# Moving the weighted-sum matmuls ahead of the second tile's transposes in each pair of attention steps

## The chip, the cores and the metric

The kernel runs on one core of a Trainium2 chip. The metric is the device time of one execution in microseconds (us). Each number of a comparison is a median over several timed runs. A profile comes from one further execution under the hardware profiler; it has a time of its own and a span (first to last instruction of the program), and all times inside the trace are counted from the span's start.

The engines are named as the profile names them: PE (matmuls) with PEld (the weight loads that go with them), DVE, ACT, POOL, and SP, which only issues DMAs here.

## The reference

The computation has two parts, one feeding the other. The first is attention whose mask comes from hashing: 4 batches with 8 heads each, 768 tokens, head size 64.

```python
q_bits = (einsum('bhsd,dk->bhsk', q, proj) > 0)      # 6 bits a token, k_bits likewise
mask = q_bucket[:, :, :, None] == k_bucket[:, :, None, :]
scores = scale * matmul(q, k.transpose(0, 1, 3, 2))
scores = where(mask, scores, -1e9)
attn = exp(scores - scores.max(-1)); attn = attn / (attn.sum(-1) + 1e-9)
attn_out = matmul(attn, v)                           # [4, 8, 768, 64]
```

The second is a mixture of 8 experts over the 3072 tokens of the attention's output (512 features): each token goes to the expert with the largest logit, through `relu(x @ w1[e]) @ w2[e]` with 1024 hidden features, and is scaled by two gate values.

## The kernel before

**Stages.** The attention runs first, as 192 *steps*. One step is one tile of 128 query rows of one head against all 768 keys. Twelve steps make a pair of heads, six of them half of its rows (three query tiles of each head). Routing of a batch (which token goes to which expert) is computed beside the next batch's attention; the experts' matmuls follow behind the attention.

**One step** consists of these parts, spread over several turns of the loop:

- *Scores* (`scores`, lines 528 and 532). PE makes 4 matmuls with 384 columns into one of two `ps_s` buffers; DVE copies the tile to `sc`, clipped, and takes each row's minimum (the scores carry a negative sign).
- *Exponential* (`soft`, line 540). ACT, in place in `sc`, with the row sums added up on the side.
- *Normalising* (`normal`, lines 547 to 550), once for two steps: DVE prepares the reciprocal of the row sums (`rsum`), POOL multiplies both tiles by it.
- *Transposes* (`transposed`, lines 561 and 562). PE turns the six 128x128 blocks of the tile, three into each of two `ps_t` buffers, and ACT copies each buffer to `pts`.
- *Weighted sums* (`weighted`, line 572). For one block `c` of 128 keys and half a pair of heads, the product of `v` with the transposed weights, one matmul for each head. The head's 64 columns fill half of the array: head 0 goes to the first 64 output rows of `ps_a`, head 1 to the other 64, and the two stand side by side. The trace shows each as two records, so the two blocks that belong to a pair of steps make eight records. Behind block 5, DVE copies `ps_a` to `ot` (line 575).

**What sets the order.** The loop is written out by hand and every engine takes its instructions in the order in which the loop issues them (`manual_schedule`); nothing reorders them later. The loop goes in pairs of steps (`GROUP = 2`). In the turn for steps s0 and s0+1 it issues the scores of these two, the transposes of s0-4 and s0-3 (`LAG = 4`), and two blocks of weighted sums, planned in the table `products`. A second table, `at`, holds what else is due behind a step: splitting and projecting the next heads, loading, the routing, and early pieces of the experts' stage. Weighted sums of a half begin two turns after its last scores, with the first blocks of `products` at step 10 and the last at step 195, so 93 turns have some.

In the text a turn's two tiles are called the first and the second: first scores, first transposes, second scores, second transposes, weighted sums is the order on PE before the change.

**Buffers that tie the engines together.** `ps_s` and `ps_t` have two buffers each. So second transposes cannot start before ACT's copies of the first transposes, and scores cannot start before DVE has read the tile of two steps earlier. `sc` has six buffers, `pts` two for each head.

Of the kernel before, what the change touches and what calls it, by code (L numbers as in the profile page):

```python
# [44 lines left out]
GROUP = 2  # L45
# [13 lines left out]
def lsh_attention_then_moe(  # L59
# [27 lines left out]
    def signed():  # L87

        for h, s in ((0, 1.0), (1, -1.0)):
            hs = slice(h * D, (h + 1) * D)  # L90
            c = 2 * NB * h
            nc.gpsimd.tensor_scalar(pjc[hs, c:c + NB], pj[hs, 0:NB], s, 0.0, ALU.mult, ALU.add)
            nc.gpsimd.tensor_scalar(pjc[hs, c + NB:c + 2 * NB], pj[hs, 0:NB], -s, 0.0, ALU.mult, ALU.add)
# [95 lines left out]
    def w2_piece(pool, r, f, idle=""):  # L189
        raw = load_weights([P, 2, DM], w2[bass.ds(expert[r], 1), :, f:f + 2].rearrange("e p f d -> p (e f) d"))  # L190
        hi, lo = split_weights(pool, "w2", NFB // 2, [P, 2, DM], raw, idle)
        return [(hi[:, j], lo[:, j]) for j in range(2)]
# [108 lines left out]
    def new_h():  # L301
        return [ep.tile([P, NFB, CAP], F32R, name=n) for n in ("hh", "hl")]
# [10 lines left out]
    def up(w1s, xs, hs, fs, n):  # L313

        ph = ps_s.tile([P, 2, 512], F32, name="ps_s")[:, 0:len(fs), 0:n]
        for j, f in enumerate(fs):
            fc = slice(f * P, (f + 1) * P)
            product(ph[:, j], [(wh[:, fc], wl[:, fc]) for wh, wl in w1s],
                    [(xs[0][:, cc, 0:n], xs[1][:, cc, 0:n]) for cc in range(NCC)])
        hh, hl = (h[:, fs[0]:fs[-1] + 1, 0:n] for h in hs)  # L320
        nc.scalar.activation(hh, ph, AF.Relu)  # L321
        return lambda: nc.vector.scalar_tensor_tensor(hl, ph, 0.0, f32(hh), ALU.max, ALU.subtract)  # L322
# [44 lines left out]
    with ExitStack() as actx:  # L367
# [11 lines left out]
        at, products = {}, {}  # L379
# [8 lines left out]
        def load(g, heads=(0, 1)):  # L388
            st = pairs[g]
            st.setdefault("qk", [])  # L390
            for j in heads:
                t = hp.tile([P, S], F32, name="qk", bufs=4)
                nc.sync.dma_start(t, qkT[2 * g + j])
                st["qk"].append(t)

        def load_v(g):
            pairs[g]["v"] = tp.tile([P, 2, NT, D], F32, name="vt", bufs=2)
            nc.sync.dma_start(pairs[g]["v"], v[g])
# [71 lines left out]
        def first_low(part):  # L470

            st = pairs[0]
            xl, yl, xr, qk = st["xl"][1], st["yl"][1], st["xr"][1], st["qk"][1]
            if part == 0:
                nc.vector.tensor_tensor(xr[D:P], qk[D:P], f32(xl[D:P]), ALU.subtract)
                nc.gpsimd.tensor_scalar(xl[D:P], qk[0:D], -0.125, 0.0, ALU.mult, ALU.add)  # L476
            else:
                nc.vector.scalar_tensor_tensor(yl[0:D], qk[0:D], -0.125, f32(xl[0:D]), ALU.mult, ALU.subtract)
# [41 lines left out]
        def scores(s):  # L520
            g, hf, t, j = tile_of(s)
            st = pairs[g]
            qs = slice(t * P, (t + 1) * P)
            ss = ps_s.tile([P, 2, 512], F32, name="ps_s")
            kb = D + 2 * NB
            for l, r, k, first in ((st["xl"][j], st["xr"][j], P, True), (st["yl"][j], st["yr"][j], kb, False)):
                for n in range(2):
                    nc.tensor.matmul(ss[:, n, 0:HS], l[0:k, qs], r[0:k, n * HS:(n + 1) * HS],  # L528
                                     start=first, stop=not first)
            sc = tp.tile([P, 2, HS], F32, name="sc", bufs=LAG + 2)  # L530
            mn = sp.tile([P, 1], F32, name="mn")
            nc.vector.tensor_scalar(sc, ss[:, :, 0:HS], MASKED, None, ALU.min, ALU.min, accum_out=mn)  # L532
            return sc, mn

        def soft(s, sc, mn):
            if s % GROUP == 0:
                sums[s // GROUP] = sp.tile([P, GROUP], F32, name="rsum")
            pr = sc.rearrange("p a b -> p (a b)")
            k = s % GROUP
            nc.scalar.activation(pr, pr, AF.Exp, bias=mn, scale=-1.0,  # L540
                                 accum_out=sums[s // GROUP][:, k:k + 1])
            return pr

        def normal(s0):

            rs = sums.pop(s0 // GROUP)
            nc.vector.tensor_scalar(rs, rs, 1e-9, None, ALU.add)
            nc.vector.reciprocal(rs, rs)  # L548
            for k in range(GROUP):
                nc.gpsimd.tensor_scalar(live[s0 + k], live[s0 + k], rs[:, k:k + 1], 0.0, ALU.mult, ALU.add)  # L550

        def transposed(s, pr):
            g, hf, t, j = tile_of(s)
            hb, t = s // 6, t - 3 * hf
            if s % 6 == 0:
                blocks[hb] = [tp.tile([P, NT, HS], F32, name=f"pts{n}") for n in range(2)]
            pts = blocks[hb][j]
            for h in range(2):
                tr = ps_t.tile([P, 3, P], F32, name="ps_t")
                for c in range(3):  # L560
                    nc.tensor.transpose(tr[:, c], pr[:, (3 * h + c) * P:(3 * h + c + 1) * P], ident)  # L561
                nc.scalar.copy(pts[:, 3 * h:3 * h + 3, t * P:(t + 1) * P], tr)  # L562
# [153 lines left out]
        for g in range(NP):  # L716
            s0 = 12 * (g - 1)
# [28 lines left out]
        s0 = 12 * (NP - 1)  # L746
# [91 lines left out]
        with tc.manual_schedule(engines=MANUAL):  # L838
            load(0)
            load(1)  # L840
            load_v(0)
            make_identity(nc, ident)

            idle = ps_t.tile([P, 3, P], F32, name="ps_t")

            def turn_idle(n):
                for i in range(n):
                    nc.tensor.transpose(idle[:, i % 3], ident, ident)

            turn_idle(14)  # L850
            first_heads()
            turn_idle(4)
            live = {}
            for s0 in range(0, NSTEP + LAG, GROUP):
                for s in range(s0, s0 + GROUP):
                    if s < NSTEP:
                        live[s] = scores(s)
                    if s < 2:
                        first_low(s)
                    if s == 1:  # L860
                        signed()
                    if 0 < s < 3:
                        turn_idle(6)
                    if s == s0 and 0 <= s - GROUP < NSTEP:
                        normal(s - GROUP)
                    if 0 <= s - LAG < NSTEP:
                        transposed(s - LAG, live.pop(s - LAG))
                    if s < NSTEP:
                        live[s] = soft(s, *live[s])
                    for fn in at.get(s, ()):  # L870
                        fn()
                for s in range(s0, s0 + GROUP):
                    for fn in products.get(s, ()):
                        fn()


            hctx.close()
            ep = ctx.enter_context(tc.tile_pool(name="ep", bufs=1, side="right", reuse_waits="tile"))
            hs = new_h()
            w2s = []  # L880
            lows = []

            def fill(f):
                lows.append(up(early["w1"], early["x"], hs, [f], CAP0))

            def low():
                lows.pop(0)()

            fill(0)
            for f in range(0, NFB, 2):  # L890
                w2s += w2_piece(ep, 0, f, "hl")
            for c in range(NT):
                weighted(2 * NP - 1, c)
                if c == 0:
                    rows(NP - 1, 0, False)
                if c == 2:
                    r["add_pair"](0, lp)
            fill(1)
            low()
            r["add_pair"](1, lp)  # L900
            fill(2)
            r["best"]()
            low()
            r["choose"]()
            rows(NP - 1, 1, False)
            fill(3)
            low()
            r["prefix"]()
            fill(4)
            r["gates"]()  # L910
            low()
            r["ranks"]()
            fill(5)
            low()
            fill(6)
            r["cols"]()
            low()
            fill(7)
            r["hot"]()
            r["table"]()  # L920
            low()
            r["entries"]()
            gid0 = lead_slots(EARLY)
            low()
# [205 lines left out]
```

## Time and profile before

| what | value |
|---|---|
| median of 3 timed runs | 796.67 us (796.37 to 797.16) |
| profiled execution: its time | 791.77 us |
| profiled execution: its span | 790.0 us |
| PE busy | 770.3 us, 98% of the span |
| DVE, ACT, POOL busy | 61%, 58%, 48% |

The attention takes about the first 462 us, the experts the rest. A matmul's end in the trace is modelled: matmuls overlap in the pipeline, and the time that one really costs is the distance from its start to the start of the next.

### The profile page before, as it was taken

How to read it: one execution, taken by the hardware profiler on the slowest of the kernel's cores; microseconds unless marked ns; L12 is line 12 of the kernel's file. 1: busy time of each engine (PE TensorE's matmuls, PEld its weight loads, DVE VectorE, ACT ScalarE, POOL GpSimd, SP SyncE). 2: the span in 40 equal slices, each digit the busy share in tenths (PEclk: the TensorE clock that was granted, in tenths of full speed). 3: DMA queues.
4: the chain of work that ended last, by engine and by line, in shares of the span. 5: the costliest groups of instructions: out<-in, count | busy, mean ns of one | idle time of the engine just before them, and what ended most of it. 6: DMA issues, size and time to landing. Idle time of an engine off the chain costs nothing. (4 is left out here: it accounts for less than half of the span.)

```text
span 790.0 us, 13715 instructions
## 1 busy us (share of the span) xinstructions
PE 770.3 (98%) x4690; PEld 608.1 (77%) x4690; DVE 479.7 (61%) x1032; ACT 459.1 (58%) x934; POOL 382.1 (48%) x422
## 2 busy tenths in 40 slices
PE   7999999999999999999999999999999999999997
PEld 6777676667676767676767658878999999988895
DVE  6676667796766896675896737236363636454640
ACT  6877777777777777777768721234151525353331
POOL 7555544444543444544445892372627273746201
PEclk9999999999999999999999999999999999999999
DMA  5554454464565456455456152363444444445601
GB/s 170 135 135 88 101 128 86 118 140 85 120 145 130 81 126 143 91 123 129 88 123 166 54 137 62 106 217 124 144 147 150 152 150 148 150 150 179 220 24 39
DMA packets 84800, 98.90 MB, mean 125 GB/s; under 512 B 57999, under 2 KB 59439, under 8 KB 84720
## 3 DMA queue, kind: packets, MB, share of 16 engines
q1 hardware_dynamic: 79376, 84.58, 41.1%
q0 software_dynamic: 5200, 13.31, 5.1%
q8 instruction: 40, 0.66, 0.3%
q14 instruction: 40, 0.33, 0.1%
q10 hardware_dynamic: 144, 0.02, 0.0%
HBM read 59.49 MB, written 13.11 MB: 92 GB/s over the span
## 5 line engine op out<-in xcount | busy, mean ns | idle before, releaser
L550 POOL TENSOR_SCALAR sc<-sc,rsum 128x768 f32<-128x768 f32 x192 | 178.9, 945 | 218.1 <-DVE rsum L548 85.8
L532 DVE TENSOR_SCALAR_CACHE_REDUCE sc<-ps_s 128x768 f32<-128x768 f32 x192 | 183.3, 955 | 96.4 <-PE ps_s L528 88.4
L562 ACT COPY pts<-ps_t 128x384 f32<-128x384 f32 x384 | 164.4, 481 | 95.5 <-PE ps_t L561 95.0
L540 ACT ACTIVATE sc<-sc,mn 128x768 f32<-128x768 f32 x192 | 181.4, 945 | 15.2 <-DVE sc L532 14.3
L561 PE MATMUL ps_t<-ident,sc 128*128 128x128 f32 x1152 | 158.4, 273 | 3.9 <-POOL sc L550 1.8
L561 PEld LDWEIGHTS ps_t<-ident,sc 128*128 128x128 f32 x1152 | 137.2, 141 | 14.3 <-POOL sc L550 4.6
L572 PE MATMUL ps_a<-pts,vt 128*64 128x384 f32 x768 | 144.8, 499 | 0.0
L528 PE MATMUL ps_s<-xr,xl 128*128 128x384 f32 x384 | 117.1, 386 | 2.4 <-POOL xl L476 2.2
L528 PEld LDWEIGHTS ps_s<-xr,xl 128*128 128x128 f32 x384 | 57.9, 190 | 71.0 <-issue 33.6
L528 PE MATMUL ps_s<-yr,yl 76*128 76x384 f32 x384 | 100.0, 341 | 0.6 <-POOL yr L438 0.5
L322 DVE SCALAR_TENSOR_TENSOR hl<-ps_s,hh 128x256 fp32r<-128x256 f32 (+8 forms) x40 | 34.0, 849 | 109.0 <-ACT hh L321 88.3
L311 PE MATMUL ps_s<-xh,w1h 128*128 128x256 f32 (+7 forms) x288 | 97.8, 340 | 2.2 <-DVE hl L322 2.1
L311 PE MATMUL ps_s<-xh,w1l 128*128 128x256 f32 (+7 forms) x288 | 96.2, 334 | 0.8 <-DVE w1l L177 0.5
L311 PE MATMUL ps_s<-xlo,w1h 128*128 128x256 f32 (+7 forms) x288 | 96.0, 333 | 0.0
L285 POOL DMA_INDIRECT xq<-x_dram,idx x75 | 82.5, 1099 | 21.6 <-issue 21.1
L328 POOL DMA_INDIRECT out_dram<-yo,sid x29 | 30.6, 1056 | 116.4 <-ACT yo L327 69.2
L572 PEld LDWEIGHTS ps_a<-pts,vt 128*64 128x64 f32 x768 | 46.7, 136 | 50.4 <-issue 47.7
L321 ACT ACTIVATE hh<-ps_s 128x256 fp32r<-128x256 f32 (+8 forms) x40 | 29.1, 727 | 90.4 <-PE ps_s L311 75.6
L528 PEld LDWEIGHTS ps_s<-yr,yl 76*128 76x128 f32 x384 | 70.4, 190 | 1.2 <-POOL yr L438 1.2
L311 PEld LDWEIGHTS ps_s<-xh,w1h 128*128 128x128 f32 x288 | 54.9, 191 | 5.8 <-DVE hl L322 3.0
L311 PEld LDWEIGHTS ps_s<-xh,w1l 128*128 128x128 f32 x288 | 54.8, 190 | 2.6 <-DVE w1l L177 0.9
L311 PEld LDWEIGHTS ps_s<-xlo,w1h 128*128 128x128 f32 x288 | 54.9, 190 | 1.1
(204 smaller groups left out, 1020.6 us busy)
## 6 DMA issues: line engine op xcount, KB each, us to landing
w_raw<-in_w_dram SPq DMA_DIRECT2D x36, 512.0 KB
qk<-in_qkT_dram SPq DMA_DIRECT2D x32, 384.0 KB
xh<-in_w_dram SPq DMA_DIRECT2D x14, 512.0 KB
xlo<-in_w_dram SPq DMA_DIRECT2D x14, 512.0 KB
vt<-in_v_dram SPq DMA_DIRECT2D x16, 384.0 KB
xr<-xl SPq DMA_DIRECT2D x30, 192.0 KB
yr<-xl SPq DMA_DIRECT2D x30, 192.0 KB
xr<-yl SPq DMA_DIRECT2D x30, 192.0 KB
```

The costliest lines, as they stand in the source:

```text
L285: nc.gpsimd.indirect_dma_start(out=xq[:, k * P:(k + 1) * P], out_offset=None, in_=x_dram.rearrange("n (a f) -> (n a) f", a=NB32), in_offse ...
L311: nc.tensor.matmul(ps, l, r, start=first and k == 0, stop=last and k == len(pairs) - 1)
L321: nc.scalar.activation(hh, ph, AF.Relu)
L322: return lambda: nc.vector.scalar_tensor_tensor(hl, ph, 0.0, f32(hh), ALU.max, ALU.subtract)
L328: nc.gpsimd.indirect_dma_start(out=out[:, :], out_offset=bass.IndirectOffsetOnAxis(ap=sid[0:n, r, a:a + 1], axis=0), in_=yo[0:n], in_offse ...
L528: nc.tensor.matmul(ss[:, n, 0:HS], l[0:k, qs], r[0:k, n * HS:(n + 1) * HS], start=first, stop=not first)
L532: nc.vector.tensor_scalar(sc, ss[:, :, 0:HS], MASKED, None, ALU.min, ALU.min, accum_out=mn)
L540: nc.scalar.activation(pr, pr, AF.Exp, bias=mn, scale=-1.0, accum_out=sums[s // GROUP][:, k:k + 1])
L550: nc.gpsimd.tensor_scalar(live[s0 + k], live[s0 + k], rs[:, k:k + 1], 0.0, ALU.mult, ALU.add)
L561: nc.tensor.transpose(tr[:, c], pr[:, (3 * h + c) * P:(3 * h + c + 1) * P], ident)
L562: nc.scalar.copy(pts[:, 3 * h:3 * h + 3, t * P:(t + 1) * P], tr)
L572: nc.tensor.matmul(st["av"][j * D:(j + 1) * D], st["v"][:, j, c], blocks[hb][j][:, c], start=(c == 0), stop=(c == NT - 1))
```

## The change

In the loop over a turn's two steps, the two blocks of weighted sums are issued in the second step, right behind its scores and ahead of its transposes. Before, they were issued behind the loop, after the second transposes and after whatever `at` holds for the second step.

```diff
                     if s == s0 and 0 <= s - GROUP < NSTEP:
                         normal(s - GROUP)
+                    if s % GROUP == GROUP - 1:
+                        for t in range(s0, s0 + GROUP):
+                            for fn in products.get(t, ()):
+                                fn()
                     if 0 <= s - LAG < NSTEP:
                         transposed(s - LAG, live.pop(s - LAG))
                     if s < NSTEP:
                         live[s] = soft(s, *live[s])
                     for fn in at.get(s, ()):
                         fn()
-                for s in range(s0, s0 + GROUP):
-                    for fn in products.get(s, ()):
-                        fn()
```

The same instructions are issued in both kernels. ACT, POOL and SP keep their order. On PE the order changes in every turn that has weighted sums. These are PE's rows of the first such turn before the change, and the scores of the next turn (`ps_s` is written by scores, `ps_t` by transposes, `ps_a` by weighted sums):

```order
L528 MATMUL ps_s<-xr,xl 128x384 x2
L528 MATMUL ps_s<-yr,yl 128x384 x2
L561 MATMUL ps_t<-ident,sc 128x128 x6
L528 MATMUL ps_s<-xr,xl 128x384 x2
L528 MATMUL ps_s<-yr,yl 128x384 x2
L561 MATMUL ps_t<-ident,sc 128x128 x6
L572 MATMUL ps_a<-pts_268,vt 64x384
L572 MATMUL ps_a<-pts_269,vt 64x384
L572 MATMUL ps_a<-pts_268,vt 64x384
L572 MATMUL ps_a<-pts_269,vt 64x384
L528 MATMUL ps_s<-xr,xl 128x384 x2
L528 MATMUL ps_s<-yr,yl 128x384 x2
```

And the same turn in the changed kernel:

```order
L528 MATMUL ps_s<-xr,xl 128x384 x2
L528 MATMUL ps_s<-yr,yl 128x384 x2
L561 MATMUL ps_t<-ident,sc 128x128 x6
L528 MATMUL ps_s<-xr,xl 128x384 x2
L528 MATMUL ps_s<-yr,yl 128x384 x2
L572 MATMUL ps_a<-pts_268,vt 64x384
L572 MATMUL ps_a<-pts_269,vt 64x384
L572 MATMUL ps_a<-pts_268,vt 64x384
L572 MATMUL ps_a<-pts_269,vt 64x384
L561 MATMUL ps_t<-ident,sc 128x128 x6
L528 MATMUL ps_s<-xr,xl 128x384 x2
L528 MATMUL ps_s<-yr,yl 128x384 x2
```

The weighted sums now stand between scores and transposes, and the next turn's first scores follow transposes.

The end of the loop, where no scores are left, reads so on PE before the change (`L311` is the first matmul of the experts' stage):

```order
L561 MATMUL ps_t<-ident,sc 128x128 x6
L572 MATMUL ps_a<-pts_5706,vt 64x384
L572 MATMUL ps_a<-pts_5707,vt 64x384
L572 MATMUL ps_a<-pts_5706,vt 64x384
L572 MATMUL ps_a<-pts_5707,vt 64x384
L561 MATMUL ps_t<-ident,sc 128x128 x12
L572 MATMUL ps_a<-pts_5706,vt 64x384
L572 MATMUL ps_a<-pts_5707,vt 64x384
L572 MATMUL ps_a<-pts_5706,vt 64x384
L572 MATMUL ps_a<-pts_5707,vt 64x384
L311 MATMUL ps_s<-xh_5571,w1h 128x256
```

and with the change:

```order
L561 MATMUL ps_t<-ident,sc 128x128 x12
L572 MATMUL ps_a<-pts_5706,vt 64x384
L572 MATMUL ps_a<-pts_5707,vt 64x384
L572 MATMUL ps_a<-pts_5706,vt 64x384
L572 MATMUL ps_a<-pts_5707,vt 64x384
L561 MATMUL ps_t<-ident,sc 128x128 x6
L311 MATMUL ps_s<-xh_5576,w1h 128x256
```

The last transposes of the attention now stand behind the last weighted sums of the loop instead of ahead of them.

On DVE the order changes in a few places only. In the turn that holds block 5, the copy of `ps_a` (L575) now stands ahead of what `at` holds for the second step. Before:

```order
L532 TENSOR_SCALAR sc,mn<-ps_s 128x768
L494 SCALAR_TENSOR_TENSOR yl<-qk,pj,xl 128x384
L575 COPY ot<-ps_a 128x384
L532 TENSOR_SCALAR sc,mn<-ps_s 128x768
L547 TENSOR_SCALAR rsum<-rsum 128x2
```

With the change:

```order
L532 TENSOR_SCALAR sc,mn<-ps_s 128x768
L575 COPY ot<-ps_a 128x384
L494 SCALAR_TENSOR_TENSOR yl<-qk,pj,xl 128x384
L532 TENSOR_SCALAR sc,mn<-ps_s 128x768
L547 TENSOR_SCALAR rsum<-rsum 128x2
```

The split of the next head's data (L494) stood ahead of the copy and now waits behind it.

## The prediction, made before the changed kernel was run

> **What bounds the kernel now.** I read the page's busy times first, then the busy times by stretch, then PE's instructions in order of time in one plain turn. From the page, and from the stretches (length, then busy time of PE, PEld, DVE, ACT and POOL, the granted clock, DMA share and rate):
>
> ```profile
> PE 770.3 (98%) x4690; PEld 608.1 (77%) x4690; DVE 479.7 (61%) x1032; ACT 459.1 (58%) x934; POOL 382.1 (48%) x422
> ...
> L572 PE MATMUL ps_a<-pts,vt 128*64 128x384 f32 x768 | 144.8, 499 | 0.0
> ...
> 31.00:449.90 418.90, 417.63 (x2749) 293.43 (x2745) 301.91 (x768) 317.00 (x729) 204.76 (x245) 1.00 0.50 117
> ```
>
> In the attention's steady part PE has 1.3 us without a matmul in 419, at the full clock. So PE bounds it, and the change moves nothing but PE's work. But a matmul's listed time overlaps its successor's, so "busy" hides what a change of kind costs. That is read from starts. One plain turn (L528 scores, L561 transposes, L572 weighted sums):
>
> ```profile
> 208.83 0.61 PE L528 MATMUL ps_s<-xr,xl 128*128 128x384 f32 x2
> ...
> 209.64 0.82 PE L561 MATMUL ps_t<-ident,sc 128*128 128x128 f32 x6
> ...
> 211.75 1.51 PE L572 MATMUL ps_a<-pts,vt 128*64 128x384 f32 x8
> 213.19 0.61 PE L528 MATMUL ps_s<-xr,xl 128*128 128x384 f32 x2
> ...
> 213.99 0.82 PE L561 MATMUL ps_t<-ident,sc 128*128 128x128 f32 x6
> 214.57 0.59 PE L528 MATMUL ps_s<-xr,xl 128*128 128x384 f32 x2
> ...
> 215.35 0.82 PE L561 MATMUL ps_t<-ident,sc 128*128 128x128 f32 x6
> 216.10 1.51 PE L572 MATMUL ps_a<-pts,vt 128*64 128x384 f32 x8
> ```
>
> From start to start: weighted sums 1.44 (211.75 to 213.19); scores behind weighted sums 0.81 and 0.80 (to 209.64, to 213.99), behind transposes 0.78 (214.57 to 215.35); transposes ahead of scores 0.58 (213.99 to 214.57), but ahead of weighted sums 0.75 (215.35 to 216.10). The turn is 0.805 + 0.58 + 0.78 + 0.75 + 1.44 = 4.355 us. The same six transposes cost 0.17 more when weighted sums follow, and the scores behind weighted sums 0.025 more. Entering and leaving the weighted sums is all that the new order can alter in PE's own pace.
>
> **The change part by part.** Nothing is removed or added, and the queues of SP and POOL keep their order. PE's order S T S T W (scores, transposes, weighted sums) becomes S T S W T. The joint T to W gives way to S to W, and W to S to W to T; the next turn's scores then follow transposes.
>
> *Entering the weighted sums.* Single starts at the joint as it is, at a scores-to-transposes joint, and, behind the loop, at a joint from the experts' matmuls (L311, of the same number type as the scores, 256 columns) to weighted sums:
>
> ```profile
> 201.84 0.27 PE L561 MATMUL ps_t<-ident,sc 128*128 128x128 f32 x1
> 202.04 0.54 PE L572 MATMUL ps_a<-pts,vt 128*64 128x384 f32 x2
> ...
> 204.12 0.34 PE L528 MATMUL ps_s<-yr,yl 76*128 76x384 f32 x1
> 204.29 0.49 PE L561 MATMUL ps_t<-ident,sc 128*128 128x128 f32 x3
> ...
> 464.66 0.28 PE L311 MATMUL ps_s<-xlo,w1h 128*128 128x256 f32 x1
> 464.78 0.28 PE L311 MATMUL ps_s<-xh,w1l 128*128 128x256 f32 x1
> 464.99 0.54 PE L572 MATMUL ps_a<-pts,vt 128*64 128x384 f32 x2
> ```
>
> The last transpose holds the weighted sums off for 0.20 us with a listed time of 0.27; the last L311 for 0.21 with 0.28, where its own kind follows after 0.12, so 0.09 more. In both the wait is the listed time less 0.07. A scores matmul is listed at 0.34 and by that gives 0.27, 0.10 more than the 0.17 after which transposes follow it. Between 0.09 and 0.10 I take 0.09, the difference read from starts alone: scores ahead of weighted sums 0.87. The joint itself is not in the trace. Its bounds are the two ends of the same row: no wait beyond the 0.17 (0.09 a turn cheaper than my value), or the whole listed 0.34 (0.17 over, 0.08 a turn dearer).
>
> The Trainium skill, TensorE: Matmul & The Clock Gate, section Single matmul latency, gives a lone warm matmul (398 + N)/2.4 ns, an estimate of 326 ns for 384 columns, 219 for 128 and 273 for 256. By that rule the weighted sums would wait 0.33 behind scores, 0.07 over my value; the turns would lose 90 x 0.025 = 2.3 us and the whole change 0.3, which is the first rival's outcome. The trace lies under the rule at 256 columns (0.21).
>
> *Leaving the weighted sums.* This joint, W to T, occurs near the end, ahead of a routing transpose (L616); the same transposes without weighted sums ahead stand below:
>
> ```profile
> 453.81 1.51 PE L572 MATMUL ps_a<-pts,vt 128*64 128x384 f32 x8
> 455.25 0.87 PE L561 MATMUL ps_t<-ident,sc 128*128 128x128 f32 x6
> 455.96 0.41 PE L616 MATMUL ps_m<-ident,lt 96*128 96x96 f32 x3
> ...
> 143.11 0.82 PE L561 MATMUL ps_t<-ident,sc 128*128 128x128 f32 x6
> 143.76 0.49 PE L616 MATMUL ps_m<-ident,lt 128*128 128x128 f32 x3
> ```
>
> The weighted sums take 1.44 ahead of transposes too; the transposes behind them 0.71 instead of 0.65, so +0.06: 0.64 ahead of scores.
>
> *A turn after the change:* 0.78 + 0.58 + 0.87 + 1.44 + 0.64 = 4.31, against 4.355: 0.045 saved. Of 768/8 = 96 groups of weighted sums three stand behind the loop and three belong to the last turns, where other things decide (below): 90 x 0.045 = 4.1 us. The bounds of the entry make it 90 x 0.135 = 12.2 saved or 90 x 0.035 = 3.2 lost.
>
> *A stall that loses its ground.* DVE's routing work delays a minimum at one place in each of three batches (the fourth wait in the first row belongs to the start):
>
> ```profile
> PE ps_t L561 <- ACT pts L562: 1.8, 4, 0.5
> ...
> 170.24 0.96 DVE L532 TENSOR_SCALAR_CACHE_REDUCE sc<-ps_s 128x768 f32<-128x768 f32 x1
> ...
> 171.24 0.94 ACT L540 ACTIVATE sc<-sc,mn 128x768 f32<-128x768 f32 x1 [1.66 <-DVE sc L532]
> 172.18 0.84 ACT L562 COPY pts<-ps_t 128x384 f32<-128x384 f32 x2
> ...
> 171.40 0.60 PE L528 MATMUL ps_s<-xr,xl 128*128 128x384 f32 x2
> 172.78 0.85 PE L561 MATMUL ps_t<-ident,sc 128*128 128x128 f32 x6 [0.42 <-ACT pts L562]
> ```
>
> ACT's exponential waits for the late minimum, the copies of the first transposes stand behind it, and the second transposes find their buffers full: 172.78 instead of 171.40 + 0.78 = 172.18, 0.60 late. In the new order weighted sums stand between: second transposes come 0.87 + 1.44 = 2.31 behind the scores, at 173.71 by this clock, and the copies are done at 172.18 + 0.84 = 173.02. Saved: 3 x 0.6 = 1.8 us, or nothing if the wait moves to the next transposes.
>
> *The end of the loop.*
>
> ```profile
> 452.24 0.62 PE L528 MATMUL ps_s<-xr,xl 128*128 128x384 f32 x2
> ...
> 201.11 0.16 DVE L547 TENSOR_SCALAR rsum<-rsum 128x2 f32<-128x2 f32 x1
> ...
> 455.57 1.03 DVE L547 TENSOR_SCALAR rsum<-rsum 128x2 f32<-128x2 f32 x1 [0.61 <-ACT sc L540]
> ...
> 455.52 1.05 POOL L174 TENSOR_SCALAR w1h<-w_raw 128x1024 fp32r<-128x1024 f32 x1
> 456.66 2.36 POOL L177 TENSOR_TENSOR w1l<-w_raw,w1h 128x1024 fp32r<-128x1024 f32 x1
> 458.99 1.81 POOL L550 TENSOR_SCALAR sc<-sc,rsum 128x768 f32<-128x768 f32 x2
> ...
> 459.96 0.87 PE L561 MATMUL ps_t<-ident,sc 128*128 128x128 f32 x6 [1.22 <-POOL sc L550]
> 463.38 0.38 PE L311 MATMUL ps_s<-xh,w1h 128*128 128x256 f32 x1
> ```
>
> PE waits 1.22 us for POOL's last normalising, so what PE saves in the last turns is lost there. DVE's `rsum` step takes 0.16 elsewhere but 1.03 here, until POOL's L174 ends. After the change the last exponential stands behind copies of transposes that start 0.87 + 1.44 after the last scores, at 454.55; with 0.58 to the copies (below), 0.86 for them and some 1.1 for the exponential it ends at 457.1, inside POOL's L177 (456.66 to 459.02). If `rsum` waits for that as it did for L174, normalising starts near 459.4, 0.4 later. From these transposes to the experts then go 0.75 + 1.44 + 0.64 = 2.83 instead of 3.42. Net 0.2 saved; bounds -0.6 and +0.4.
>
> The Trainium skill, SBUF — State Buffer, says of the port pair that DVE and GpSimd share that whichever starts first holds it for the whole instruction. The 1.03 agrees; without the rule the term would be 0.6 saved.
>
> *Costed at nothing.* The copy of `ps_a` ahead of L494 holds DVE until the weighted sums end, 3.7 us into the turn, plus 0.3; copy and split then take until 5.1, and the next minimum can start only 1.1 behind the next scores, at 5.4. Without that cover a projecting turn would lose up to 1.0. The second tile's exponential comes some 1.5 later: behind it waits `rsum`, which in DVE's order stands behind the next minimum anyway, and normalised tiles are wanted two turns on.
>
> *Sum:* 4.1 + 1.8 + 0.2 = 6.1 us. The profiled execution would take 785.7 instead of 791.77, of which 783.9 in the span instead of 790.0. It is 4.9 under the median of the timed runs, which I take as common to both kernels: 796.67 - 6.1 = 790.6 us.
>
> **The rivals.**
>
> *Scores drain fully* before weighted sums enter. For it: that joint is unseen, and its matmuls are the longest. Against: L311. The entry costs 0.08 more, the turns lose 3.2, the rest saves 2.0: 797.9 us, 0.15% over, no change.
>
> *No wait at all* behind scores. For it: scores to transposes has none. Against: both entries seen have one. 796.67 - 12.2 - 2.0 = 782.5 us.
>
> *Slower: the second transposes' copies come late.* In the new order second transposes are followed 0.64 + 0.78 later by the next turn's first transposes, which need their `ps_t` buffers. The copies stand on ACT behind the first tile's exponential.
>
> ```profile
> 204.58 0.96 DVE L532 TENSOR_SCALAR_CACHE_REDUCE sc<-ps_s 128x768 f32<-128x768 f32 x1 [2.04 <-PE ps_s L528]
> 204.82 0.86 ACT L562 COPY pts<-ps_t 128x384 f32<-128x384 f32 x2 [0.90 <-PE ps_t L561]
> 205.58 0.94 ACT L540 ACTIVATE sc<-sc,mn 128x768 f32<-128x768 f32 x1
> ```
>
> The scores of this minimum start 0.81 ahead of the transposes of 204.29, at 203.48, so the minimum starts 1.1 and the exponential ends 3.0 into the turn; the copies want ACT 0.78 + 0.58 + 0.87 + 1.44 = 3.67 into the turn and 0.58 later, at 4.25 (0.53 from 204.29 above to 204.82, and the 0.05 by which transposes behind weighted sums start slower). The case decides once DVE is over 1.1 us late. For it: DVE is busy 301.91 of 418.90 us here and has been that late at three places. Against: the margin. At the seen price of 0.6 in a third of the turns: 30 x 0.6 - 6.1 = 11.9 lost, 808.6 us.
>
> **How the numbers follow.** Forecast 0.76, full drain 0.11, no wait 0.05, late copies 0.08. 0.2% is 1.6 us, about what a measurement of this kernel can tell from no change. The forecast's own range, 788 to 794, is faster but for 0.02 of it: faster 0.74 + 0.05 = 0.79, same 0.02 + 0.11 = 0.13, slower 0.08. The range takes in the bounds of the entry, 782.5 to 797.9, and leaves out the late copies.
>
> **What would show it.** In the changed trace: 0.27 from the last start of scores to the first of weighted sums (0.17 or 0.34 for the first two rivals); weighted sums to transposes 1.44; a plain turn near 4.31; no wait on `pts` at the routing's three places; at the end `rsum` held until L177 ends. Waits of transposes on ACT or POOL in many turns, or a plain turn no shorter than 4.35, would make the prediction wrong.

## The result

The changed kernel is faster: 787.28 us (784.19 to 788.05) against 796.37 (792.03 to 797.16), a ratio of 0.9902 with a 95% interval of 0.9877 to 0.9928. Timed again in a later comparison, both kernels on one chip, it took 786.16 against 792.60, a ratio of 0.992 (0.9897 to 0.9944). By the ratios that is 7.8 and 6.3 us (by the first comparison's medians 9.1); the forecast was 6.1. The kernel before has medians from 788.63 to 796.37 over the comparisons below, about as far apart as the change is worth. So a kernel is set against the kernel before of its own comparison, and kernels of different comparisons only by these ratios. The ratios are of fast executions; one slow one, 1238 us at a granted clock of 0.557, of the kernel called "kernel before, two differences less", is left out of its ratio.

The profiled execution took 788.05 us with a span of 786.3, against 791.77 and 790.0: only 3.7 less. Where the rest went is a part of what follows.

**The plain turn.** PE's instructions in order of time in the profile after (start, length, engine, line, operation, operands, count):

```profile
206.52 0.60 PE L528 MATMUL ps_s<-xr,xl 128*128 128x384 f32 x2
...
207.31 0.82 PE L561 MATMUL ps_t<-ident,sc 128*128 128x128 f32 x6
207.89 0.60 PE L528 MATMUL ps_s<-xr,xl 128*128 128x384 f32 x2
...
208.76 1.51 PE L572 MATMUL ps_a<-pts,vt 128*64 128x384 f32 x8
210.20 0.88 PE L561 MATMUL ps_t<-ident,sc 128*128 128x128 f32 x6
210.83 0.59 PE L528 MATMUL ps_s<-xr,xl 128*128 128x384 f32 x2
```

Scores 0.79, transposes 0.58, scores ahead of weighted sums 0.87, weighted sums 1.44, transposes behind them 0.63: 4.31 us, where the prediction had 0.78, 0.58, 0.87, 1.44, 0.64. The single starts at the joint that no trace of before contained:

```profile
212.80 0.34 PE L528 MATMUL ps_s<-yr,yl 76*128 76x384 f32 x1
213.06 0.54 PE L572 MATMUL ps_a<-pts,vt 128*64 128x384 f32 x1
```

0.26 us, between the 0.17 of no wait and the 0.34 of a full drain. Over the 90 such joints of this trace's attention the median wait is 0.264 with a listed time of 0.333: "listed time less 0.07", as at the two joints that the trace of before contained.

**The routing's place.** The same three scores, weighted sums and transposes where second transposes waited before (the kernel before at 172.78), and ACT there:

```profile
170.13 0.59 PE L528 MATMUL ps_s<-xr,xl 128*128 128x384 f32 x2
...
171.00 1.51 PE L572 MATMUL ps_a<-pts,vt 128*64 128x384 f32 x8
172.45 0.87 PE L561 MATMUL ps_t<-ident,sc 128*128 128x128 f32 x6
...
170.97 0.84 ACT L562 COPY pts<-ps_t 128x384 f32<-128x384 f32 x2
```

ACT's copies end at 171.81; the transposes come at 172.45 without a wait. PE's waits of transposes for ACT (in all, how many, the longest), and the stretch from the first weighted sums to the last scores, in which PE is without a matmul for 0.15 us (1.3 before, in the prediction's row):

```profile
PE ps_t L561 <- ACT pts L562: 0.9, 2, 0.5
...
29.72:447.02 417.30, 417.15 (x2779) 288.14 (x2778) 297.73 (x775) 318.03 (x738) 208.63 (x247) 1.00 0.51 118
```

Of the four waits before, the one at the start is left, and one of 0.33 us is new, behind the last scores (at 449.93). The 0.15 are new too: at 440.49, in one of the last turns, transposes wait for a normalising of POOL's that stands behind an L177, a difference of the experts' weights. They come 1.10 behind their scores there instead of 0.79.

**The end of the loop.** The last scores start at 446.39 and the experts' first matmul at 457.12, 10.73 us later; before it was 463.38 - 452.24 = 11.14. DVE, POOL and PE:

```profile
446.39 0.61 PE L528 MATMUL ps_s<-xr,xl 128*128 128x384 f32 x2
...
451.13 1.76 DVE L547 TENSOR_SCALAR rsum<-rsum 128x2 f32<-128x2 f32 x1 [2.19 <-ACT sc L540]
...
450.49 2.36 POOL L177 TENSOR_TENSOR w1l<-w_raw,w1h 128x1024 fp32r<-128x1024 f32 x1
453.28 1.79 POOL L550 TENSOR_SCALAR sc<-sc,rsum 128x768 f32<-128x768 f32 x2 [0.42 <-DVE lgt L618]
...
457.12 0.36 PE L311 MATMUL ps_s<-xh,w1h 128*128 128x256 f32 x1
```

`rsum` is held for 1.76 us and ends at 452.89, with L177 (450.49 + 2.36 = 452.85), as the prediction's last turn had it. Normalising starts 453.28 - 446.39 = 6.89 behind the last scores, before 458.99 - 452.24 = 6.75. It now follows 0.43 behind the end of L177, before directly; but L177 itself ends 6.46 behind the last scores, before 6.78 (459.02). From normalising to the experts' first matmul go 3.84 instead of 4.39.

**Behind the attention**, where the prediction saw nothing, the changed kernel loses time. DVE's choice of experts for the last batch, POOL beside it, and the prefix sums (L673) that wait for it, after:

```profile
466.44 1.63 DVE L634 TENSOR_TENSOR df<-lgt,mx 128x48 f32<-128x48 f32 x1
468.34 0.74 DVE L642 TENSOR_SCALAR eq<-df 128x48 f32<-128x48 f32 x1
...
469.59 2.02 DVE L646 TENSOR_TENSOR oneh<-ei,expi 128x48 f32<-128x48 f32 x1
...
465.64 2.38 POOL L177 TENSOR_TENSOR w2l<-w_raw,w2h 128x1024 fp32r<-128x1024 f32 x1
467.98 1.05 POOL L174 TENSOR_SCALAR w2h<-w_raw 128x1024 fp32r<-128x1024 f32 x1
469.11 2.43 POOL L177 TENSOR_TENSOR w2l<-w_raw,w2h 128x1024 fp32r<-128x1024 f32 x1
...
471.88 0.20 PE L673 MATMUL ps_m<-ohb,tri 128*128 128x48 bf16 x1 [1.68 <-DVE ohb L649]
```

and before:

```profile
472.73 0.58 DVE L634 TENSOR_TENSOR df<-lgt,mx 128x48 f32<-128x48 f32 x1
473.56 2.21 DVE L642 TENSOR_SCALAR eq<-df 128x48 f32<-128x48 f32 x1
...
476.28 0.21 DVE L646 TENSOR_TENSOR oneh<-ei,expi 128x48 f32<-128x48 f32 x1
...
472.20 1.05 POOL L174 TENSOR_SCALAR w2h<-w_raw 128x1024 fp32r<-128x1024 f32 x1
...
476.77 0.20 PE L673 MATMUL ps_m<-ohb,tri 128*128 128x48 bf16 x1 [1.33 <-DVE ohb L649]
```

L634 and L646 end when an L177 of POOL ends (468.07 and 468.02; 471.61 and 471.54), and L642 when L174 does (469.08 and 469.03). Before, two steps of this chain met a POOL step, L634 an L174 (473.31 and 473.25) and L642 an L177; after, three do. The three steps together take 4.39 us instead of 3.00. That is the whole loss: from the experts' first matmul to the prefix sums PE needs 471.88 - 457.12 = 14.76 instead of 476.77 - 463.38 = 13.39. So the profiled gain runs 5.85 at the last scores, 6.26 at the experts' first matmul, 4.89 at the prefix sums, and 3.7 at the span's end. The last 1.2 are waits of PE on expert weights. The second profile of the same kernel (span 783.6) has few of these, but a longer wait for the gathered tokens; single profiles do not settle them.

### The profile page after: what moved, and what is told of

Its sections match the earlier page's. It is cut to its first block, busy times and chain, and to the rows that moved or that the text cites. A ratio compares the mean times of both kernels' runs of the same rounds, so it can differ in the third digit from the quotient of the medians.

```text
span 786.3 us, 13715 instructions
## 1 busy us (share of the span) xinstructions
PE 765.4 (97%) x4690; PEld 599.6 (76%) x4690; DVE 474.1 (60%) x1032; ACT 456.1 (58%) x934; POOL 380.4 (48%) x422
## 5 line engine op out<-in xcount | busy, mean ns | idle before, releaser
L561 PEld LDWEIGHTS ps_t<-ident,sc 128*128 128x128 f32 x1152 | 130.4, 141 | 63.5 <-POOL sc L550 50.8
L561 PE MATMUL ps_t<-ident,sc 128*128 128x128 f32 x1152 | 163.8, 278 | 2.6 <-POOL sc L550 1.6
L528 PE MATMUL ps_s<-xr,xl 128*128 128x384 f32 x384 | 115.0, 380 | 2.2 <-POOL xl L476 2.2
L311 PE MATMUL ps_s<-xh,w1h 128*128 128x256 f32 (+7 forms) x288 | 97.8, 340 | 3.8 <-DVE hl L322 3.2
L311 PE MATMUL ps_s<-xh,w1l 128*128 128x256 f32 (+7 forms) x288 | 96.1, 334 | 0.8 <-DVE w1l L177 0.8
L311 PE MATMUL ps_s<-xlo,w1h 128*128 128x256 f32 (+7 forms) x288 | 95.9, 333 | 0.8 <-issue 0.8
L311 PEld LDWEIGHTS ps_s<-xh,w1h 128*128 128x128 f32 x288 | 55.0, 191 | 6.4 <-DVE hl L322 2.4
L311 PEld LDWEIGHTS ps_s<-xh,w1l 128*128 128x128 f32 x288 | 54.8, 190 | 3.1 <-DVE w1l L177 1.6
L311 PEld LDWEIGHTS ps_s<-xlo,w1h 128*128 128x128 f32 x288 | 54.9, 191 | 1.6 <-issue 0.5
```

The source lines that it names most:

```text
L311: nc.tensor.matmul(ps, l, r, start=first and k == 0, stop=last and k == len(pairs) - 1)
```

## The experiments

The theory (of joints): on PE, entering the weighted sums and leaving them has a price that depends on what stands before and behind, and the new order has the cheaper joints. The main rival (of the place): the gain comes from giving ACT time between second scores and second transposes, whatever the joints.

| kernel | median us | before, same comparison | ratio (95% interval) |
|---|---|---|---|
| changed kernel, again | 786.16 | 792.60 | 0.9920 (0.9897 to 0.9944) |
| weighted sums behind first scores | 783.12 | 788.63 | 0.9925 (0.9904 to 0.9947) |
| weighted sums behind first transposes | 783.30 | 788.63 | 0.9927 (0.9906 to 0.9947) |
| one block behind each scores | 809.95 | 788.63 | 1.0275 (1.0240 to 1.0309) |
| projection and logits joined | 779.56 | 788.63 | 0.9879 (0.9857 to 0.9901) |
| no block, four and two blocks in three turns | 791.09 | 792.60 | 0.9983 (0.9967 to 0.9999) |
| weight halves on ACT | 789.63 | 792.60 | 0.9963 (0.9942 to 0.9984) |
| joined, and weight halves on ACT | 785.53 | 792.60 | 0.9920 (0.9896 to 0.9944) |
| changed kernel, two differences less | 784.16 | 794.21 | 0.9871 (0.9846 to 0.9896) |
| kernel before, two differences less | 792.92 | 794.21 | 0.9978 (0.9957 to 0.9998) |
| joined, last differences on DVE | 781.71 | 794.21 | 0.9846 (0.9825 to 0.9868) |

### The same joints at another place

```diff
-                    if s % GROUP == GROUP - 1:
+                    if s == s0:
                         for t in range(s0, s0 + GROUP):
```

> Weighted sums stand behind the first scores of a turn and ahead of the first transposes (S W T S T). The joints on PE are the same as in the changed kernel, scores to weighted sums and weighted sums to transposes, but at another place. Theory of joints: a plain turn takes 4.31 us as in the changed kernel, against 4.355 before, and the time is 6 to 8 us under the kernel before. Rival, that the place counts because ACT gets time between second scores and second transposes: a plain turn stays at 4.35 and the time is within 2 us of before.

PE's order of this kernel:

```profile
210.53 0.59 PE L528 MATMUL ps_s<-xr,xl 128*128 128x384 f32 x2
...
211.41 1.51 PE L572 MATMUL ps_a<-pts,vt 128*64 128x384 f32 x8
212.85 0.87 PE L561 MATMUL ps_t<-ident,sc 128*128 128x128 f32 x6
213.48 0.60 PE L528 MATMUL ps_s<-xr,xl 128*128 128x384 f32 x2
...
214.27 0.82 PE L561 MATMUL ps_t<-ident,sc 128*128 128x128 f32 x6
214.85 0.60 PE L528 MATMUL ps_s<-xr,xl 128*128 128x384 f32 x2
```

210.53 to 214.85 is 4.32, the same single steps as in the changed kernel (0.88, 1.44, 0.63, 0.79, 0.58), and the time is 0.75% under before (5.9 us, expected 6 to 8). For a turn's pace the place does not count; the joints do. The routing's wait is a matter of place, and it is gone here as well: PE has no wait at all between the first weighted sums and the last scores. So some 1.8 of the 5.9 us are that wait, here as in the changed kernel.

### The old joints at another place

The block of weighted sums now stands in the first step, behind its transposes (the diff, like all here but where it is said otherwise, is against the changed kernel):

```diff
-                    if s % GROUP == GROUP - 1:
-                        for t in range(s0, s0 + GROUP):
-                            for fn in products.get(t, ()):
-                                fn()
                     if 0 <= s - LAG < NSTEP:
                         transposed(s - LAG, live.pop(s - LAG))
+                    if s == s0:
+                        for t in range(s0, s0 + GROUP):
+                            for fn in products.get(t, ()):
+                                fn()
```

> Weighted sums stand behind the first transposes and ahead of the second scores (S T W S T). The joints are those of the kernel before, transposes to weighted sums and weighted sums to scores, at another place. Theory of joints: a plain turn takes 4.35 us; only the wait on ACT at the routing's three places goes, since the two transposes stand further apart: about 2 us under before, 4 us over the changed kernel. Rival of the place: the turn is shorter than 4.35 and the time is that of the changed kernel.

The plain turn is as the theory of joints has it, 4.35 (198.75 to 203.10 below, scores to the end of weighted sums), but the time is 5.8 us under before where 2 were expected: that of the kernel above, as the rival had it. The expectation overlooked what the loop issues next: behind the first step stands `at`, with the projection of the next heads (L406) and the routing's logits, whose matmuls fill 32 of the array's columns. A turn of before with the projection in it begins here and ends at the 208.83 of the prediction's rows:

```profile
203.48 0.62 PE L528 MATMUL ps_s<-xr,xl 128*128 128x384 f32 x2
```

The plain turn of this run, and what stands behind its weighted sums:

```profile
198.75 0.61 PE L528 MATMUL ps_s<-xr,xl 128*128 128x384 f32 x2
...
201.66 1.51 PE L572 MATMUL ps_a<-pts,vt 128*64 128x384 f32 x8
203.10 0.85 PE L406 MATMUL ps_m<-qk,pjc 128*32 128x384 f32 x8
203.88 0.62 PE L528 MATMUL ps_s<-xr,xl 128*128 128x384 f32 x2
```

Before, such a turn paid the 0.17 by which transposes are dearer ahead of column blocks a second time, and scores behind column blocks twice. Here L406 follows the weighted sums directly and costs 0.78 (203.10 to 203.88) and nothing besides: these turns are 5.13 us (198.75 to 203.88), 0.22 less than the 5.35 of before, in 23 turns 5.1 us. With the 1.8 of the routing's wait, which is gone here too, that would be 6.9; 5.8 were measured, with an interval from 4.2 to 7.6. So the time alone does not decide between theory and rival here. The turns do: the plain one kept its length with the old joints, and the ones with L406 lost a joint and became shorter, an effect that was not foreseen.

### Each joint twice

```diff
-                    if s % GROUP == GROUP - 1:
-                        for t in range(s0, s0 + GROUP):
-                            for fn in products.get(t, ()):
-                                fn()
+                    for fn in products.get(s, ()):
+                        fn()
```

> Each of a turn's two blocks of weighted sums stands behind the scores of its own step (S W T S W T), so that each joint is there twice. Theory of joints: an entry costs 0.09, the transposes behind 0.05 more, and two short blocks of four records 0.80 each instead of one of 1.44, together 0.30 a turn: 4.60 us a turn, 90 x 0.25 = 22 us over before less the 2 of the routing's wait, some 816. Rival, that entering and leaving costs next to nothing and the gain lies in who waits for whom: within 3 us of the changed kernel.

```profile
217.59 0.59 PE L528 MATMUL ps_s<-xr,xl 128*128 128x384 f32 x2
...
218.48 0.87 PE L572 MATMUL ps_a<-pts,vt 128*64 128x384 f32 x4
219.27 0.88 PE L561 MATMUL ps_t<-ident,sc 128*128 128x128 f32 x6
219.90 0.60 PE L528 MATMUL ps_s<-xr,xl 128*128 128x384 f32 x2
```

Half a turn takes 219.90 - 217.59 = 2.31, a turn 4.62 (4.60 expected), and the kernel is 2.75% over before: 21.7 us, expected 20. Entering and leaving weighted sums costs PE 0.3 us a time: 0.09 and 0.05 at its two joints, as expected, and 0.15 within the block, since two blocks of four records take 0.79 each and one of eight 1.44. Nothing else grew: the attention has 0.2 us of waits in all.

### Joining what also fills only some columns

The projection (planned two steps into a pair of heads) and the logits go into a table `beside` and are issued right ahead of `products`:

```diff
                     if s % GROUP == GROUP - 1:
+                        for t in range(s0, s0 + GROUP):
+                            for fn in beside.get(t, ()):
+                                fn()
                         for t in range(s0, s0 + GROUP):
                             for fn in products.get(t, ()):
```

> As the changed kernel, but the projection of the next heads (L406) and the routing's logits (L606), whose matmuls also fill only some of the array's columns and which stand alone behind first transposes in 23 turns, now stand right ahead of that turn's weighted sums. Theory of joints: one entry and one exit less in each of these turns; L406 costs 2 x 0.32 = 0.64 us there instead of the 0.98 by which such turns are longer now, 0.34 x 23 = 7.8 us under the changed kernel, about 780. If going from 32-column to 64-column blocks is a joint of its own, less than half of that. Rival of the place: no difference from the changed kernel.

```profile
39.02 0.85 PE L407 MATMUL ps_m<-qk,pjc 128*32 128x384 f32 x8
39.81 1.51 PE L573 MATMUL ps_a<-pts,vt 128*64 128x384 f32 x8
```

(The lines are one higher here.) L406 takes 0.79 ahead of the weighted sums, as long as ahead of scores (0.78), not the expected 0.64. So only its two outer joints are saved, and going from blocks of 32 columns to blocks of 64 has a price too, 0.15 by an estimate: L406's eight records are two groups of four, and if a group takes the 0.32 by which two more records lengthen a block of weighted sums, two take 0.64. Such turns are 5.09 instead of 5.28, 0.19 x 23 = 4.4 us; by the ratios the kernel is 0.46% under the one with weighted sums behind first scores (3.6 us). That is a gain, by the ratios in the lower branch of the expectation (less than half of 7.8), by the turns just over it.

### Fewer joints

```diff
-                    products.setdefault(12 * g + 6 * hf + 6 + LAG + c, []).append(lambda hb=2 * g + hf, c=c: weighted(hb, c))
+                    products.setdefault(12 * g + 6 * hf + 6 + LAG + max(c, 2), []).append(lambda hb=2 * g + hf, c=c: weighted(hb, c))
```

> As the changed kernel, but of a half's three turns the first has no weighted sums, the second four blocks and the third two. One entry and one exit less in three turns: by the joints alone 30 x 0.30 = 9 us under the changed kernel. Rival, that ACT becomes the bound: a turn without weighted sums takes 0.78 + 0.58 + 0.78 + 0.58 = 2.7 us on PE, but ACT needs two exponentials of 1.1 and four copies of 0.43, 4.0 us; transposes then wait for copies in that turn, at least 0.6 us where the wait at the routing was seen, and 30 x 1.2 or so is lost against the 9: 20 to 30 us over the changed kernel.

```profile
209.76 0.60 PE L528 MATMUL ps_s<-xr,xl 128*128 128x384 f32 x2
...
210.65 0.84 PE L561 MATMUL ps_t<-ident,sc 128*128 128x128 f32 x6
211.25 0.60 PE L528 MATMUL ps_s<-xr,xl 128*128 128x384 f32 x2
...
212.32 0.85 PE L561 MATMUL ps_t<-ident,sc 128*128 128x128 f32 x6
...
213.80 2.80 PE L572 MATMUL ps_a<-pts,vt 128*64 128x384 f32 x16
216.53 0.88 PE L561 MATMUL ps_t<-ident,sc 128*128 128x128 f32 x6
```

The rival was right in sign and wrong in size. In the turn without weighted sums transposes come 0.89 and then 1.07 behind the start of their scores instead of 0.78. ACT has no idle time there, and these transposes start 0.63 and 0.64 behind the start of the two copies that free their buffers (210.02 and 211.68), much as at the routing's place before (172.18 to 172.78). This eats the 0.3 of the saved entry and exit (three turns in a row, from the scores at 208.39 to those at 221.47, take 13.08 us; three of the changed kernel's 4.31 are 12.93), and at the routing's three places scores wait 0.8 for DVE. (The sixteen records take 2.73, eight more than 1.44 by 1.29: 0.16 a record, and 0.15 for the block once.) The kernel loses 0.6% against the changed one (by the ratios 0.9983 and 0.9920), 5 us where 20 to 30 were expected.

### What is lost behind the attention

Five runs ask whether DVE is held there by POOL. First the rounded halves of the weights on ACT:

```diff
-                w2s += w2_piece(ep, 0, f, "hl")
+                w2s += w2_piece(ep, 0, f, "l")
```

> As the changed kernel, but the rounded halves of the first expert's second weights (four steps of 1.05 us on POOL, L174, behind the attention) are made by ACT; POOL keeps the differences (four of 2.4 us, L177). If DVE's routing steps of the last batch are held by POOL's differences, as the trace suggests (steps of 0.2 and 0.6 us that take 1.5 and 2.0 until an L177 ends), POOL is done about 4 us earlier, fewer of these fall on the routing, and the stretch from the experts' first matmul to the routing's prefix sums (14.8 us in the changed kernel, 13.4 before) loses 1 to 1.5 us: as much in the time. Rival, that the routing there is slow because its matmuls come late: no change. If ACT's copies wait for weights that are still loading, ACT's later work waits behind them and the kernel is slower by up to 2 us.

> The projection and the logits right ahead of the weighted sums (which measured 0.19 us saved in each of 23 turns) together with the weight halves on ACT. If the two are independent: 4.4 us under the changed kernel and the other step's 1 to 1.5 besides, 10 to 12 us under before. If the second step brings nothing: as without it, 9 under before.

Both are slower than without it, by the ratios 3.4 and 3.2 us: the third case of the first expectation in kind, with more than its 2 us, and none of the second's cases. ACT waits for the loading of the third and fourth weights (the third's row is below, for the fourth 2.04 us), and its work for the experts' first layer stands behind; from the experts' first matmul to the prefix sums go 17.3 us:

```profile
466.12 1.05 ACT L176 CAST w2h<-w_raw 128x1024 fp32r<-128x1024 f32 x1 [5.59 <-DMA w_raw<-in_w_dram]
...
465.85 0.21 DVE L634 TENSOR_TENSOR df<-lgt,mx 128x48 f32<-128x48 f32 x1
```

The one useful row is the last: with POOL idle at that moment, L634 takes 0.21 instead of 1.63. Then POOL's last two differences are left out, in both kernels (the two low parts are set to zero beforehand):

```diff
-                w2s += w2_piece(ep, 0, f, "hl")
+                if f == 4:
+                    los = [ep.tile([P, 2, DM], F32R, name="w2l", bufs=NFB // 2) for _ in range(2)]
+                    for lo in los:
+                        nc.gpsimd.memset(f32(lo), 0.0)
+                if f < 4:
+                    w2s += w2_piece(ep, 0, f, "hl")
+                else:
+                    raw = load_weights([P, 2, DM], w2[bass.ds(expert[0], 1), :, f:f + 2].rearrange("e p f d -> p (e f) d"))
+                    hi, lo = ep.tile([P, 2, DM], F32R, name="w2h", bufs=NFB // 2), los.pop(0)
+                    nc.gpsimd.tensor_scalar(hi, raw, 1.0, 0.0, ALU.mult, ALU.add)
+                    w2s += [(hi[:, j], lo[:, j]) for j in range(2)]
```

> The changed kernel without two of POOL's four differences behind the attention (L177, 2.4 us each): the low parts of the last two pieces of the first expert's second weights are set to zero beforehand and not computed, so its output lacks that small correction. Theory, that the changed kernel loses 1.3 us there because POOL's differences fall on DVE's routing steps: DVE's steps L634, L642 and L646 take their 0.2 us, the stretch from the experts' first matmul to the prefix sums falls from 14.7 to 13 us or less. Rival, that the routing waits for something else there: the stretch stays at 14.7.

> The kernel before without the same two differences, as the control: its stretch of 13.4 has only one held step, so it falls by less. Theory: with the differences gone in both, the two stretches are equal to 0.2 us, and the changed kernel lies under this one by what the attention alone saves, 90 x 0.046 + 1.9 + 0.4 = 6.4 us. Rival: the stretch of the changed kernel stays over a microsecond longer.

From the experts' first matmul to the prefix sums the changed kernel now needs 469.35 - 457.12 = 12.23 us instead of 14.76, the one before 474.93 - 463.31 = 11.62 instead of 13.39. So the held steps are the cause of the loss: the difference of the two falls from 1.37 to 0.61, where 0.2 was expected, and these 0.61 are again a held step. L634 takes 0.94 us in this kernel and 0.34 in its control, both times until the POOL step ends that makes a rounded half and was not removed:

```profile
466.44 0.94 DVE L634 TENSOR_TENSOR df<-lgt,mx 128x48 f32<-128x48 f32 x1
467.64 0.17 DVE L642 TENSOR_SCALAR eq<-df 128x48 f32<-128x48 f32 x1
```

The distance of the two kernels in time is 1.07% (8.5 us), more than the 6.4 expected, but each interval is some 2 us wide to either side.

A version that computes everything lets DVE make the last two differences, behind the routing's ranks and behind its columns, with projection and logits joined:

```diff
...
+                nc.gpsimd.tensor_scalar(hi, raw, 1.0, 0.0, ALU.mult, ALU.add)
+                w2s += [(hi[:, j], lo[:, j]) for j in range(2)]
+                late_lo.append(lambda lo=lo, raw=raw, hi=hi: nc.vector.tensor_tensor(lo, raw, f32(hi), ALU.subtract))
...
             r["ranks"]()
             fill(5)
             low()
+            late_lo.pop(0)()
             fill(6)
             r["cols"]()
             low()
+            late_lo.pop(0)()
```

> A version that computes everything: projection and logits right ahead of the weighted sums, and the last two differences made by DVE (1.22 us each, as it makes them for the later experts) behind the routing's ranks and columns instead of by POOL ahead of them. Theory of the held steps: DVE gets back about 3.5 us of held steps and pays 2.4 later, 1 us under the version with projection and logits alone, about 10 us under before. Rival, that DVE's chain to the gather of the tokens is what counts and pays the 2.4 in full: 1 us over that version.

It has the lowest ratio here, 781.71 against 794.21: 1.54% under before (12.2 us). Over the joined version's 1.21% that is 0.33%, 2.6 us, but the two stand in different comparisons and their intervals overlap. In the profiles the stretch from the experts' first matmul to the prefix sums falls from 14.37 in the joined version to 12.25, as the theory of the held steps has it.

### The changed kernel again

> The changed kernel once more, timed on the same chip and against the same runs of the kernel before as the other three. The prediction's sum gives 6.1 us under before; the joints and the routing's wait as its trace shows them, 90 x 0.046 + 1.9 = 6.0, less 1.4 that its trace loses again behind the attention, 4.6. A chip that makes the first comparison's 9 us would mean a gain that neither trace shows.

6.3 us by the ratio, 4.4 to 8.2 by its interval. The sum's 6.1 and the first comparison's 7.8 both lie inside. So do the 4.6 us that the first trace leaves over when the loss behind the attention is taken off, so the timing alone does not decide whether that loss belongs to every execution. The profile of this run has the loss again: L634, L642 and L646 take 1.59, 0.73 and 2.01 us, and from the experts' first matmul to the prefix sums go 14.66.

## Why the prediction was right

- **The joints.** Right in kind and size: 0.27 predicted, 0.26 measured; transposes 0.64 and 0.63; the turn 4.31 and 4.31. One experiment puts the new joints at another place (4.32), one the old joints (4.35), and one has each joint twice and pays 0.3 us a time: each turn is as long as its joints ask for.
- **The routing's wait.** Right, 3 x 0.6: second transposes that came 0.60 late now come at 172.45, 1.45 behind the weighted sums at 171.00, which is these matmuls' own pace. Of PE's 1.3 us without a matmul in the steady part 0.15 are left, none of them at these places, so the wait did not move to the next transposes either.
- **The end of the loop.** Right in mechanism: `rsum` is held until L177 ends. Mis-sized: normalising comes 0.14 later by its scores, not 0.4, since L177, which the prediction left at its place, ends 0.32 sooner behind the last scores. The way from there to the experts is 0.55 shorter (0.59 predicted), so 0.41 is saved, not 0.2, just past the bound of 0.4.
- **What was costed at nothing.** Held but for one place: the copy and the split that it delays cost PE no wait. The one new wait between the first weighted sums and the last scores is at 440.49, 0.15 by the profile and 0.3 from start to start, and comes from POOL, where the prediction looked for none.
- **What was missing.** The step that took everything behind the end of the loop for a mere shift. DVE's last routing meets POOL's weight differences at other moments; that took back 1.4 and 1.3 us in the two profiles of the changed kernel, and waits behind it another 1.2 in the first. The joints, the wait and the end of the loop come to 6.26 in the trace, as forecast; the span gained 3.7, and the timings say 7.8 and 6.3, each uncertain by 2. That 6.1 lies so near to the timed gains although it lacks this loss is in part luck, and why the timings show more than the profile stays open. The first comparison's median, 787.28, is under the forecast's own range of 788 to 794 and within the wider one; the kernel before was 0.3 faster there than in the timing that the forecast started from.
- **The rivals.** The full drain would have needed 0.34, no wait 0.17; neither is there. The Trainium skill, TensorE: Matmul & The Clock Gate, section Single matmul latency, gives the latency of a lone bf16 matmul; used as the wait at this joint it would have given 0.33. The measured 0.26, on matmuls that the rows list as f32, decides against using it so. Late copies did not come in the changed kernel; they came where PE's turn was made shorter than ACT's work (the turn without weighted sums), at 0.11 and 0.29 us rather than 0.6.

## What to carry to other kernels

When an engine is busy 98% of the time, look at the distance between starts, block by block: a block that costs 0.17 us more ahead of one neighbour than ahead of another shows a joint, and reordering alone can save part of it. Add up the joints of the new order too: here the old pair cost 0.17 and 0.025, the new one 0.09 and 0.05, so 0.05 of the 0.17 was saved. On PE, matmuls that use only part of the array's columns were cheapest kept together and entered behind long matmuls (0.09) rather than behind transposes (0.17); leaving them cost 0.025 ahead of scores and 0.05 ahead of transposes. Scores on both sides were not tried. Moving the block was worth 0.8 to 1.0%, about two thirds of it by the joints and the rest by a wait that lost its ground; joining two kinds brought 0.4 to 0.5% more. Ask also what later work a shift runs into: a short DVE step that fell between two long ones of POOL may now fall on one and last until its end.

## What was unexpected of the hardware

- Changing from 32-column to 64-column blocks on PE costs about 0.15 us by the estimate above, half of what going between full and partial columns costs in and out (0.3). The Trainium skill, TensorEngine Tiling (Array Packing), section Key Properties, states that changing the tiling mode, not just the tile, drains TensorE. The runs agree that each such change has a price and that transposes and scores, which both use all columns, have none between them (0.58 from the transposes' start to the scores', the pace without a joint). They do not show a drain of the whole listed time: 0.26 us behind scores listed at 0.34.
- At such a change the load of the new weights (PEld) does not run ahead of its matmul. In the kernel before, the first load of the weighted sums starts at 202.04 with its matmul (202.04), that of transposes behind scores 0.17 ahead of it (204.29 in the prediction's rows):

```profile
202.04 0.20 PEld L572 LDWEIGHTS ps_a<-pts,vt 128*64 128x64 f32 x4 [0.17 <-issue]
...
204.12 0.75 PEld L561 LDWEIGHTS ps_t<-ident,sc 128*128 128x128 f32 x6
```

  At every joint of the attention between full and partial columns, in both kernels and both ways, the load starts at most 0.003 us ahead. Whether the late load makes the joint dear, or both wait for the same thing, no run here separates.
- A DVE step of 0.2 us on 48 columns can take 1.5 to 2.2 us while POOL subtracts two tiles in SBUF, even where it handles as little as 128x48. The cost to DVE is what is left of POOL's step, so a shift of a microsecond decides how many steps of a chain are held, and for how long (L634 took 1.63 with L177 running, 0.58 near the end of an L174, and 0.21 with POOL idle).
